# A decode layer in one kernel: the third value product moved ahead of the gate's sum, and the last three rows of w_out in four quarters

## The chip, the cores and the metric

The kernel runs on one core of a Trainium2 chip. The metric is the device time of one execution in microseconds (us), and the figure compared is the median of several runs. A profile is taken of one further execution. Its span, from the first to the last instruction, is shorter than that execution's time, because the time also holds what lies around the program.

## What is computed

One token goes through two branches in parallel, and both results are added to the input. Branch A is attention over the last 4096 positions of a cache with 32 query heads and 16 key and value heads. Branch B is a gated MLP whose gate is normalised over its 2304 values.

```python
xn = _layernorm(x, axis=-1)                       # x: 1 x 1 x 576, bfloat16
return x + _A_ref(xn, k_cache, v_cache, wq, wo) + _B_ref(xn, w_in, w_sp, b_sp, w_out)

# A: W = 4096, 16 heads of 128, each shared by two query heads
q = (xn @ wq).reshape(1, 1, 32, 128)
p = softmax(q . k[last W] * 128 ** -0.5)
A = (p . v[last W]).reshape(1, 1, 4096) @ wo      # wo: 4096 x 576

# B: F/2 = 2304
z = gelu(xn @ w_in)                               # w_in: 576 x 4608
g = w_sp * layernorm(z[..., 2304:]) + b_sp
B = (z[..., :2304] * g) @ w_out                   # w_out: 2304 x 576
```

## The kernel before, in words

All weights and the used part of both caches, 51 MB, are read once. SyncE's queue (SP) issues these loads in a fixed order: wq, k0, k1, v0, k2, v1, k3, win, v2, v3, wo (two parts: rows 0 to 19 and 20 to 31), wout (four parts: rows 0 to 8, 9 to 14, 15 and 16, 17). They share two pools of two buffers each: the small one holds k0, k1, k2, k3, v2 and wout in turn, the large one wq, v0, v1, win, v3 and wo. A load is issued when its buffer is free: wo (L92) when the product with win has been made, wout when k3 has been transposed.

The order of work on each engine is the order in which the program text lists it; no scheduler moves anything. The heads are worked on in four groups of four (b = 0 to 3):

- `turn(b)` (L209): VectorE transposes the group's keys.
- `scores(b)`: TensorE multiplies them with the query (L254), VectorE adds a mask and takes the maximum (L257 to L270), ScalarE takes the exponential (L274), VectorE transposes the probabilities (L276), TensorE sums them (L278, L280).
- `values(b)`: TensorE multiplies the probabilities with the values, 32 matmuls in four column groups into one PSUM tile `pv` (L288). ScalarE copies it to `pvs` (L293). Eight matmuls add up the parts (`op`, L296) and VectorE scales the result into `o_t` (L299).

Then comes branch B. `z_all` multiplies with win in four column groups (L311), and VectorE copies and transposes the result (L315, L317). `gate` is a chain of some fifteen short VectorE and ScalarE operations (L325 to L348), with one matmul in its middle that sums two columns over the partitions (`sz_ps`, L341). Its result `hv` holds 18 columns, one for each row of w_out. The lines around the change are these:

```python
    scores(3)
    gate(z_all())
    values(2)
    values(3)
```

So on TensorE the gate's sum L341 stands ahead of the third values' products, and behind it come the third and the fourth values.

At the end o_t is transposed and reordered into `o_p` (L366 to L370), and all products that make the output are accumulated in PSUM: `row_of` (L376) multiplies one column with one row of weights of 576 values, as two matmuls of 288 columns, the first half into `fin[0]` (partition 0), the second into `fin[1]` (partition 32). It is called once for the input x, 32 times for wo and 18 times for wout, where each part of wout is waited for by the first row that needs it (rows 0, 9, 15 and 17). VectorE casts the one half to bfloat16 (L388), ScalarE the other (L389), and each is written out by a transfer of its own: SP's queue (L390) and ScalarE's queue (L391).

A row (PE) of the profile that says 128*1 is a matmul with 128 partitions and one active column; PEld is the load of that column ahead of it.

Of the kernel before, what the change touches and what calls it, by code (L numbers as in the profile page):

```python
# [8 lines left out]
FP32 = mybir.dt.float32  # L9
BF16 = mybir.dt.bfloat16  # L10
ALU = mybir.AluOpType
# [3 lines left out]
P = 128  # L15
D = 576
# [16 lines left out]
FR = FH // P  # L33
WR = HQ * DH // P
HW = D // 2
ZPAD = 24
ZW = P + ZPAD
SMALL = NU * DH
# [4 lines left out]
def kernel(  # L43
# [14 lines left out]
    nc = tc.nc  # L58
    ctx.enter_context(tc.manual_schedule())

    const = ctx.enter_context(tc.tile_pool(name="const", bufs=1))
    work = ctx.enter_context(tc.tile_pool(name="work", bufs=2))
    one = ctx.enter_context(tc.tile_pool(name="one", bufs=1))
# [7 lines left out]
    ps_a = ctx.enter_context(tc.tile_pool(name="ps_a", bufs=2, space=PS))  # L71
# [11 lines left out]
    def unit(name, width):  # L83
        pool = small if width == SMALL else large
        return pool.tile([P, width], BF16, name=name, tag="u")
# [32 lines left out]
    wout_t = unit("wout", SMALL)  # L118
# [52 lines left out]
    def rstd_of(stats_ps, n, name):  # L171
        mv = const.tile([P, 4], FP32, name=name)
        nc.vector.tensor_scalar_mul(mv[:, 0:2], stats_ps, 1.0 / n)
        nc.vector.tensor_mul(mv[:, 2:3], mv[:, 0:1], mv[:, 0:1])
        nc.vector.tensor_sub(mv[:, 2:3], mv[:, 1:2], mv[:, 2:3])
        nc.scalar.activation(mv[:, 2:3], mv[:, 2:3], ACT.Ln, bias=eps_t[:, 0:1])
        nc.scalar.activation(mv[:, 3:4], mv[:, 2:3], ACT.Exp, scale=-0.5)
        return mv
# [37 lines left out]
    for r in range(NR):  # L216
        for g in range(4):
            nc.tensor.matmul(q_ps[32 * g:32 * g + 32, :], lhsT=xw[:, r, :],  # L218
                             rhs=wq_t[:, 2048 * r + 512 * g:2048 * r + 512 * (g + 1)],
                             start=r == 0, stop=r == NR - 1, tile_position=(0, 32 * g))  # L220
# [5 lines left out]
    for g in range(4):  # L226
        nc.tensor.matmul(qr[:, :, g, :], lhsT=rep4[:, g, :, :].rearrange("p n q -> p (n q)"),
                         rhs=qT[:, :, 0:2, :].rearrange("p a h e -> p h a e"), start=True, stop=True)
    for b in range(NB):
        half, y = divmod(b, 2)  # L230
        nc.vector.tensor_tensor(
            out=zq[:, b, :, ZPAD:].rearrange("p c (n x) -> p c n x", n=4)[:, :, :, 0:8],
            in0=qr[:, half, 2 * y:2 * y + 2, :].rearrange("p g (x c) -> p c (g x)", c=4).unsqueeze(2)
            .to_broadcast([P, 4, 4, 8]),
            in1=qm[:].unsqueeze(1).unsqueeze(3).to_broadcast([P, 4, 4, 8]), op=ALU.mult)
# [10 lines left out]
    def scores(b):  # L246
        sm = one.tile([P, 2, 512], FP32, name=f"sm{b}", tag="sm")
        mx = work.tile([P, 2], FP32, name=f"mx{b}", tag="mx")
        for kk in range(2):
            s_ps = ps_s.tile([P, 512], FP32, name=f"s{b}_{kk}", tag="s")  # L250
            for k4 in range(4):
                for ce in range(4):
                    c, e = divmod(ce, 2)
                    nc.tensor.matmul(s_ps[:], lhsT=zq[:, b, ce, ZPAD - 8 * k4:ZPAD - 8 * k4 + P],  # L254
                                     rhs=kt[b, 4 * kk + k4][:, c, :, e],
# [23 lines left out]
        rms[b] = work.tile([P, 8], FP32, name=f"rm{b}", tag="rm")  # L279
        nc.vector.reciprocal(rms[b][:], su[:])  # L280

    def values(b):
        pv = ps_v.tile([P, 512], FP32, name=f"pv{b}", tag="pv")
        v4 = vn[b][:, 0:NU * DH].rearrange("p (k n u d) -> p k u n d", k=2, n=4, d=DH)
        for kk in range(2):
            for u in range(UK):
                g = u % 4
                nc.tensor.matmul(  # L288
                    pv[32 * g:32 * g + 32, :].rearrange("p (n d) -> p n d", n=4), lhsT=p_t[b][:, kk, u, :],
                    rhs=v4[:, kk, u, :, :], start=kk == 0 and u < 4, stop=kk == 1 and u >= UK - 4,  # L290
                    tile_position=(0, 32 * g))
        pvs = one.tile([P, 512], FP32, name=f"pvs{b}", tag="pvs")
        nc.scalar.copy(pvs[:], pv[:])  # L293
        op = ps_m.tile([P, 8], FP32, name=f"op{b}", tag="m")
        for u in range(4):
            nc.tensor.matmul(op[:], lhsT=pvs[:, DH * u:DH * (u + 1)], rhs=selu[:, 8 * u:8 * u + 8],  # L296
                             start=u == 0, stop=u == 3)
        with nc.allow_low_precision(reason="the attention's output is bfloat16 in the reference"):
            nc.vector.tensor_tensor(out=o_t[:, 8 * b:8 * b + 8], in0=op[:], in1=rms[b][:], op=ALU.mult)  # L299


    hv = const.tile([P, FR], BF16, name="hv")

    def z_all():
        zs = one.tile([P, D], FP32, name="zs", tag="sm")
        zp = [ps_a.tile([P, HW], FP32, name=f"z{i}", tag="a") for i in range(2)]
        for r in range(NR):
            for g in range(4):
                for i in range(2):
                    a = D * g + HW * i  # L310
                    nc.tensor.matmul(zp[i][32 * g:32 * g + 32, :], lhsT=xw[:, r, :],  # L311
                                     rhs=win_t[:, FH * r + a:FH * r + a + HW],
                                     start=r == 0, stop=r == NR - 1, tile_position=(0, 32 * g))
        for i in range(2):
            nc.vector.tensor_copy(zs[:, HW * i:HW * (i + 1)], zp[i][:])  # L315
        zt = one.tile([P, FR, 32], FP32, name="zt", tag="zt")
        nc.vector.transpose(zt[:], zs[:].rearrange("p (i r) -> p r i", r=FR))  # L317
        return zt[:, :, 0:2]

    def gate(z):  # L320
        def t3(name):
            return const.tile([P, FR, 2], FP32, name=name)

        u = t3("u")
        nc.vector.tensor_mul(u[:], z, z)  # L325
        nc.vector.tensor_scalar(out=u[:], in0=u[:], scalar1=0.044715, scalar2=1.0, op0=ALU.mult, op1=ALU.add)
        nc.vector.tensor_mul(u[:], u[:], z)
        nc.vector.tensor_scalar_max(u[:], u[:], -50.0)
        e = t3("e")
        nc.scalar.activation(e[:], u[:], ACT.Exp, scale=-2.0 * GELU_C)  # L330
        nc.vector.tensor_scalar_add(e[:], e[:], 1.0)
        nc.vector.reciprocal(e[:], e[:])
        G = const.tile([P, 2, FR], FP32, name="G")
        nc.vector.tensor_mul(G[:].rearrange("p h c -> p c h"), e[:], z)
        sz = const.tile([P, 2], FP32, name="sz")
        nc.vector.tensor_reduce(out=sz[:, 0:1], in_=G[:, 1, :], axis=AXX, op=ALU.add)
        jz = const.tile([P, FR], FP32, name="jz")
        nc.vector.tensor_tensor_reduce(out=jz[:], in0=G[:, 1, :], in1=G[:, 1, :], scale=1.0, scalar=0.0,
                                       op0=ALU.mult, op1=ALU.add, accum_out=sz[:, 1:2])
        sp = ps_m.tile([P, 2], FP32, name="sz_ps", tag="m")  # L340
        nc.tensor.matmul(sp[:], lhsT=ones_f[:], rhs=sz[:], start=True, stop=True)  # L341
        mz = rstd_of(sp[:], FH, "mz")
        gz = const.tile([P, FR], FP32, name="gz")
        nc.vector.tensor_scalar(out=gz[:], in0=G[:, 1, :], scalar1=mz[:, 0:1], scalar2=mz[:, 3:4],
                                op0=ALU.subtract, op1=ALU.mult)
        nc.vector.tensor_scalar(out=gz[:], in0=gz[:], scalar1=wb[:, 0:1], scalar2=wb[:, 1:2],
                                op0=ALU.mult, op1=ALU.add)
        nc.vector.tensor_mul(hv[:], G[:, 0, :], gz[:])  # L348
# [3 lines left out]
    turn(1)  # L352
    scores(1)
    values(0)
    turn(2)
    scores(2)
    values(1)
    turn(3)
    scores(3)
    gate(z_all())  # L360
    values(2)
    values(3)


# [4 lines left out]
    o_p = const.tile([P, WR], BF16, name="o_p")  # L369
    nc.vector.tensor_copy(o_p[:], op_ps[:])  # L370

    fin = [ps_s.tile([P, HW], FP32, name=f"fin{g}", tag="s") for g in range(2)]

    def row_of(col, w, start=False, stop=False):
        for g in range(2):
            nc.tensor.matmul(fin[g][32 * g:32 * g + 1, :], lhsT=col, rhs=w[:, HW * g:HW * (g + 1)],  # L376
                             start=start, stop=stop, tile_position=(0, 32 * g))

    row_of(one_bf[:, 0:1], x_row, start=True)
    for r in range(WR):  # L380
        row_of(o_p[:, r:r + 1], wo_t[:, D * r:D * (r + 1)])
    for r in range(FR):
        row_of(hv[:, r:r + 1], wout_t[:, D * r:D * (r + 1)], stop=r == FR - 1)


    y = out.flatten_outer_dims()
    res = [const.tile([P, HW], BF16, name=f"res{g}") for g in range(2)]
    nc.vector.tensor_copy(res[0][0:1, :], fin[0][0:1, :])  # L388
    nc.scalar.copy(res[1][32:33, :], fin[1][32:33, :])  # L389
    nc.sync.dma_start(y[:, 0:HW], res[0][0:1, :])  # L390
    nc.scalar.dma_start(y[:, HW:D], res[1][32:33, :])  # L391

# [1 line left out]
_INS = ['A_x', 'A_k_cache', 'A_v_cache', 'A_wq', 'A_wo', 'B_x', 'B_w_in', 'B_w_sp', 'B_b_sp', 'B_w_out']  # L394
# [26 lines left out]
```

## Time and profile before

| what | value |
|---|---|
| time, median of 3 runs | 127.47 us (127.39 to 127.73) |
| time of the profiled execution | 127.53 us |
| span of the profiled execution | 125.7 us |
| mean granted TensorE clock | 0.81 |
| busy: PE, PEld, VectorE (DVE), ScalarE (ACT) | 78.6, 37.6, 64.3, 10.2 us |
| HBM read over the span | 50.96 MB, 405 GB/s |

An engine's busy time is summed over its instructions. The clock is the share of full speed that the throttle granted TensorE. In the timeline, the first column is the start of a group of instructions in us from the span's start, the second how long it lasted; brackets hold the idle time of the engine before it and what ended that. In the chain of waits, each piece of time is given to what the end of the program waited for. In a table of stretches, each engine's busy time comes with the number of its instructions, then the granted clock, the share of the 16 DMA engines and the GB/s.

These lines are from the timeline around the work that the first edit moves:

```profile
92.25 3.82 PE L311 MATMUL z<-win,xw 128*32 128x288 bf16 x72
...
100.63 0.59 PE L341 MATMUL sz_ps<-sz,ones_f 128*128 128x2 f32 x2 [4.55 <-DVE sz L338]
...
101.15 3.60 PE L288 MATMUL pv<-v,pt 128*32 128x512 bf16 x32
...
104.80 0.58 ACT L293 COPY pvs<-pv 128x512 f32<-128x512 f32 x1 [2.44 <-PE pv L288]
...
105.44 1.88 PE L296 MATMUL op<-selu,pvs 128*128 128x8 f32 x8 [0.69 <-ACT pvs L293]
...
107.25 3.30 PE L288 MATMUL pv<-v,pt 128*32 128x512 bf16 x32
```

TensorE ends z at about 96.1 us, idles 4.55 us until the gate's sum, and then does the third and the fourth values, one behind the other.

### The profile page before, as it was taken

Reading aid. Unit: us, or ns where it says so; the run is one execution under the profiler, and the core shown is the slowest. Engines: PE = TensorE matmul, PEld = TensorE weight load, DVE = VectorE, ACT = ScalarE, POOL = GpSimd, SP = SyncE. Lnnn points to the kernel's source line nnn. Section 1 sums busy time; section 2 is a strip of 40 time slices with the busy share of each in tenths; the row PEclk is TensorE's granted clock in tenths of the full one; section 3 lists DMA queues with packets and bytes.
Section 4 is the critical chain, followed back from the end, with each engine's and each line's share of the span. In section 5 each row is a group of like instructions: output and inputs, shape, how many; then the busy total and the mean of one; then the engine's idle time right before and its main releaser. Section 6 shows DMA issues by size and latency. Waiting matters only on the chain.

```text
span 125.7 us, 1318 instructions
## 1 busy us (share of the span) xinstructions
PE 78.6 (62%) x534; PEld 37.6 (30%) x534; DVE 64.3 (51%) x129; ACT 10.2 (8%) x19; POOL 3.9 (3%) x10
## 2 busy tenths in 40 slices
PE   0042750099823998297599646699375097969861
PEld 0032220034211333145234223234063044435540
DVE  6315233499839995330999451999444830010001
ACT  2101000000030000301000031000120011010001
POOL 8400000000000000000000000000000000000000
PEclk9999998559996589755559999689976855595899
DMA  4999899998999989899898999999899999999950
GB/s 102 515 420 438 382 480 438 396 490 365 480 427 394 480 365 490 386 448 469 375 480 386 497 422 422 414 397 480 386 459 443 386 432 442 393 430 411 411 207 0
DMA packets 2467, 51.03 MB, mean 406 GB/s; under 512 B 284, under 2 KB 414, under 8 KB 670
## 3 DMA queue, kind: packets, MB, share of 16 engines
q1 hardware_dynamic: 2450, 50.96, 95.0%
q8 instruction: 4, 0.07, 0.2%
q14 instruction: 1, 0.01, 0.0%
q10 hardware_dynamic: 12, 0.00, 0.0%
HBM read 50.96 MB, written 0.00 MB: 405 GB/s over the span
## 4 chain that ended last, share of the span: by engine, by line
PE 43%; DMA 37%; DVE 10%; ACT 5%; SPq 2%; issue 1%; ACTq 0%
PE s L254 30%; DMA wout<-in_B_w_out_dram 19%; DMA k<-in_A_k_cache_dram 18%; PE pv L288 4%; ACT p L274 4%; DVE kt L209 4%; PE z L311 3%; PE op L296 2%; DVE sm L257 2%; PE tr L265 2%; SPq L92 2%; PE fin L376 1%; PE su L278 1%; DVE pt L276 1%; DVE m L267 1%
## 5 line engine op out<-in xcount | busy, mean ns | idle before, releaser
L254 PE MATMUL s<-kt,zq 128*128 128x512 bf16 x128 | 37.2, 456 | 11.1 <-DVE kt L209 11.1
L209 DVE STREAM_TRANSPOSE kt<-k 128x1024 f32<-128x1024 f32 x32 | 36.4, 1205 | 3.9 <-DMA k<-in_A_k_cache_dram 3.9
L254 PEld LDWEIGHTS <-zq 128*128 128x128 bf16 x128 | 14.4, 112 | 32.8 <-issue 22.1
L288 PE MATMUL pv<-v,pt 128*32 128x512 bf16 x128 | 12.4, 557 | 0.0
L274 ACT ACTIVATE p<-sm,nm 128x1024 bf16<-128x1024 f32 x4 | 4.6, 1147 | 67.9 <-DVE nm L270 67.9
L299 DVE TENSOR_TENSOR o_t<-op,rm 128x8 bf16<-128x8 f32 x4 | 0.7, 166 | 17.2 <-PE op L296 17.2
L276 DVE STREAM_TRANSPOSE pt<-p 128x1024 bf16<-128x1024 bf16 x4 | 5.0, 1245 | 5.4 <-ACT p L274 5.4
L296 PE MATMUL op<-selu,pvs 128*128 128x8 f32 x32 | 5.9, 311 | 2.9 <-ACT pvs L293 2.9
L257 DVE CUSTOM_DVE_ANT_1 sm<-s,cm 128x512 f32<-128x512 f32 x8 | 5.4, 671 | 3.7 <-PE s L254 3.7
L296 PEld LDWEIGHTS op<-selu,pvs 128*128 128x128 f32 x32 | 5.5, 259 | 5.8 <-ACT pvs L293 5.8
L278 PE MATMUL su<-sel,l 128*128 128x8 f32 x8 | 1.8, 293 | 7.6 <-ACT p L274 7.6
L218 PE MATMUL q_ps<-wq,xw 128*32 128x512 bf16 x36 | 4.2, 626 | 3.0 <-DVE xw L187 2.4
L376 PE MATMUL fin<-wo,o_p 128*1 128x288 bf16 x64 | 5.8, 357 | 0.1
L156 PE MATMUL x_ps<-one_bf,x_row 1*64 1x1 bf16 x9 | 1.2, 248 | 7.4 <-DMA x_row<-in_A_x_dram 7.4
L288 PEld LDWEIGHTS <-pt 128*32 128x32 bf16 x128 | 4.0, 128 | 5.6 <-issue 4.8
L388 DVE CAST res<-fin 1x288 bf16<-1x288 f32 x1 | 0.4, 446 | 9.9 <-PE fin L376 9.9
L265 PE MATMUL tr<-ident_f,m 128*128 128x128 f32 x8 | 1.9, 326 | 3.9 <-DVE m L263 3.9
L376 PEld LDWEIGHTS <-o_p 128*1 128x1 bf16 x64 | 3.4, 103 | 2.3 <-DVE o_p L370 0.3
L278 PEld LDWEIGHTS su<-sel,l 128*128 128x128 f32 x8 | 1.4, 218 | 8.4 <-ACT p L274 8.4
L311 PE MATMUL z<-win,xw 128*32 128x288 bf16 x72 | 3.8, 392 | 0.0
L376 PE MATMUL fin<-wout,hv 128*1 128x288 bf16 x36 | 2.6, 285 | 1.5 <-DMA wout<-in_B_w_out_dram 1.5
L293 ACT COPY pvs<-pv 128x512 f32<-128x512 f32 x4 | 2.3, 585 | 14.3 <-PE pv L288 14.3
(88 smaller groups left out, 39.0 us busy)
## 6 DMA issues: line engine op xcount, KB each, us to landing
k<-in_A_k_cache_dram SPq DMA_DIRECT2D x4, 4096.0 KB
v<-in_A_v_cache_dram SPq DMA_DIRECT2D x4, 4096.0 KB, 39.0
win<-in_B_w_in_dram SPq DMA_DIRECT2D x1, 5184.0 KB
wq<-in_A_wq_dram SPq DMA_DIRECT2D x1, 3584.0 KB
wo<-in_A_wo_dram SPq DMA_DIRECT2D x1, 2880.0 KB
wo<-in_A_wo_dram SPq DMA_DIRECT2D x1, 1728.0 KB, 20.0
wout<-in_B_w_out_dram SPq DMA_DIRECT2D x1, 1296.0 KB
wq<-in_A_wq_dram SPq DMA_DIRECT2D x1, 1024.0 KB, 4.9
```

Source lines behind the costliest of these rows:

```text
L209: nc.vector.transpose(t[:].rearrange("p c n e -> p (c n e)").bitcast(FP32), kn[b][:, UK * DH * k:UK * DH * (k + 1)].bitcast(FP32).rearrang ...
L218: nc.tensor.matmul(q_ps[32 * g:32 * g + 32, :], lhsT=xw[:, r, :], rhs=wq_t[:, 2048 * r + 512 * g:2048 * r + 512 * (g + 1)], start=r == 0, ...
L254: nc.tensor.matmul(s_ps[:], lhsT=zq[:, b, ce, ZPAD - 8 * k4:ZPAD - 8 * k4 + P], rhs=kt[b, 4 * kk + k4][:, c, :, e], start=k4 == 0 and ce = ...
L257: nc.vector.tensor_tensor_reduce(out=sm[:, kk, :].rearrange("p (n s) -> p n s", s=HB), in0=s_ps[:].rearrange("p (n s) -> p n s", s=HB), in ...
L265: nc.tensor.matmul(tr[:], lhsT=m1[:].to_broadcast([P, P]), rhs=ident_f[:], start=True, stop=True)
L274: nc.scalar.activation(p[:], sm[:].rearrange("p k n -> p (k n)"), ACT.Exp, bias=nm[:], accum_out=l[:])
L276: nc.vector.transpose(p_t[b][:].rearrange("p k u m -> p (k u m)"), p[:])
L278: nc.tensor.matmul(su[:], lhsT=l[:].to_broadcast([P, P]), rhs=sel8[:], start=True, stop=True)
L288: nc.tensor.matmul(pv[32 * g:32 * g + 32, :].rearrange("p (n d) -> p n d", n=4), lhsT=p_t[b][:, kk, u, :], rhs=v4[:, kk, u, :, :], start=k ...
L296: nc.tensor.matmul(op[:], lhsT=pvs[:, DH * u:DH * (u + 1)], rhs=selu[:, 8 * u:8 * u + 8], start=u == 0, stop=u == 3)
L311: nc.tensor.matmul(zp[i][32 * g:32 * g + 32, :], lhsT=xw[:, r, :], rhs=win_t[:, FH * r + a:FH * r + a + HW], start=r == 0, stop=r == NR - ...
L376: nc.tensor.matmul(fin[g][32 * g:32 * g + 1, :], lhsT=col, rhs=w[:, HW * g:HW * (g + 1)], start=start, stop=stop, tile_position=(0, 32 * g))
```

## The change

`values` is split into `weigh` (the products and ScalarE's copy) and `heads` (the eight matmuls and the scaling). For group 2, `weigh` is called between `z_all` and `gate`, and `heads` behind `gate`. Groups 0, 1 and 3 keep both together.

The last three rows of w_out (LATE = 3: rows 15, 16 and 17) no longer accumulate into `fin`. Its accumulation stops at row 14. The four quarters of `fin`, 144 columns each, are copied into a tile `sums` in SBUF, at partitions 0, 32, 64 and 96: two copies on VectorE, two on ScalarE. The three rows are multiplied in four quarters each, twelve matmuls of 144 columns in four column groups, into a tile `last` in PSUM at the same four partitions. One VectorE operation over 128 partitions adds the two tiles and casts to bfloat16; both tiles are filled with zeros before, as only four of their partitions are written. Each of the two output transfers now writes two rows of 144 values (288 bytes), taken from two partitions.

```diff
-    def values(b):
+    def weigh(b):
         pv = ps_v.tile([P, 512], FP32, name=f"pv{b}", tag="pv")
...
         nc.scalar.copy(pvs[:], pv[:])
+        return pvs
+
+    def heads(b, pvs):
         op = ps_m.tile([P, 8], FP32, name=f"op{b}", tag="m")
...
+    def values(b):
+        heads(b, weigh(b))
...
-    gate(z_all())
-    values(2)
+    z = z_all()
+    pvs2 = weigh(2)
+    gate(z)
+    heads(2, pvs2)
     values(3)
...
+    last = ps_a.tile([P, QW], FP32, name="last", tag="a")
+    nc.vector.memset(last[:], 0.0)
+    sums = one.tile([P, QW], FP32, name="sums", tag="pvs")
+    nc.vector.memset(sums[:], 0.0)
...
-    for r in range(FR):
-        row_of(hv[:, r:r + 1], wout_t[:, D * r:D * (r + 1)], stop=r == FR - 1)
...
-    nc.vector.tensor_copy(res[0][0:1, :], fin[0][0:1, :])
-    nc.scalar.copy(res[1][32:33, :], fin[1][32:33, :])
-    nc.sync.dma_start(y[:, 0:HW], res[0][0:1, :])
-    nc.scalar.dma_start(y[:, HW:D], res[1][32:33, :])
+    for r in range(FR - LATE):
+        row_of(hv[:, r:r + 1], wout_t[:, D * r:D * (r + 1)], stop=r == FR - LATE - 1)
+    for c in range(2):
+        nc.vector.tensor_copy(sums[32 * c:32 * c + 1, :], fin[0][0:1, QW * c:QW * (c + 1)])
+        nc.scalar.copy(sums[64 + 32 * c:65 + 32 * c, :], fin[1][32:33, QW * c:QW * (c + 1)])
+    for r in range(FR - LATE, FR):
+        for c in range(4):
+            nc.tensor.matmul(last[32 * c:32 * c + 1, :], lhsT=hv[:, r:r + 1],
+                             rhs=wout_t[:, D * r + QW * c:D * r + QW * (c + 1)],
+                             start=r == FR - LATE, stop=r == FR - 1, tile_position=(0, 32 * c))
+
+    y = out.flatten_outer_dims().rearrange("o (c n) -> (o c) n", c=4)
+    res = const.tile([P, QW], BF16, name="res")
+    nc.vector.tensor_tensor(out=res[:], in0=last[:], in1=sums[:], op=ALU.add)
+    nc.sync.dma_start(y[0:2, :], res[0:64:32, :])
+    nc.scalar.dma_start(y[2:4, :], res[64:128:32, :])
```

More of the change, by code (lines that the diff above doesn't have):

```diff
@@ L35 @@
 HW = D // 2
+QW = D // 4
+LATE = 3
 ZPAD = 24
@@ L381 @@
         row_of(o_p[:, r:r + 1], wo_t[:, D * r:D * (r + 1)])
-    for r in range(FR):
-        row_of(hv[:, r:r + 1], wout_t[:, D * r:D * (r + 1)], stop=r == FR - 1)
[L386 to L390, printed above, removed]
-    nc.scalar.dma_start(y[:, HW:D], res[1][32:33, :])
+    for r in range(FR - LATE):
[13 more added lines that the diff above has]
+    nc.scalar.dma_start(y[2:4, :], res[64:128:32, :])
 _INS = ['A_x', 'A_k_cache', 'A_v_cache', 'A_wq', 'A_wo', 'B_x', 'B_w_in', 'B_w_sp', 'B_b_sp', 'B_w_out']
```

## The prediction

> **What bounds the kernel now.** I read the page's queue table first, then the chain of work that ended last, then the tail of the timeline.
>
> ```profile
> DMA packets 2467, 51.03 MB, mean 406 GB/s; under 512 B 284, under 2 KB 414, under 8 KB 670
> ## 3 DMA queue, kind: packets, MB, share of 16 engines
> q1 hardware_dynamic: 2450, 50.96, 95.0%
> q8 instruction: 4, 0.07, 0.2%
> ```
>
> SP's queue (q1) keeps 16 engines busy for 95% of the span: the kernel is one stream of 51 MB. The chain from 90 us on shows where it ends:
>
> ```profile
> 92.33 3.81 PE z L311 x72
> ...
> 97.48 24.29 DMA wout<-in_B_w_out_dram
> 121.78 0.04 issue
> 121.82 1.39 PE fin L376 x18
> 123.21 0.43 DVE res L388
> ```
>
> Between 97.5 and 121.8 only w_out's transfer stands on the path. What PE, VectorE and ScalarE do there is off it while it is done before the part of w_out that it needs. The tail, from the timeline:
>
> ```profile
> 113.32 5.76 PE L376 MATMUL fin<-wo,o_p 128*1 128x288 bf16 x64
> ...
> 119.71 1.27 PE L376 MATMUL fin<-wout,hv 128*1 128x288 bf16 x18 [0.64 <-DMA wout<-in_B_w_out_dram]
> ...
> 121.82 1.35 PE L376 MATMUL fin<-wout,hv 128*1 128x288 bf16 x18 [0.84 <-DMA wout<-in_B_w_out_dram]
> ...
> 123.20 0.45 DVE L388 CAST res<-fin 1x288 bf16<-1x288 f32 x1 [9.94 <-PE fin L376]
> 123.23 0.39 ACT L389 CAST res<-fin 1x288 bf16<-1x288 f32 x1 [11.99 <-PE fin L376]
> ...
> 123.67 0.31 SPq L390 DMA_DIRECT2D out_dram<-res  x1
> ```
>
> PE waits 0.64 us for rows 0 to 8 and 0.84 us for rows 9 to 17. The second group is 0.08 us longer than the first although it is the same work; the stretches of 0.04 us show why (columns: PE, PEld, DVE, ACT, POOL, clock, DMA):
>
> ```profile
> 122.50:122.54 0.04, 0.04 (x4) 0.01 (x1) 0.00 (x0) 0.00 (x0) 0.00 (x0) 1.00 0.00 0
> 122.54:122.58 0.04, 0.04 (x4) 0.00 (x0) 0.00 (x0) 0.00 (x0) 0.00 (x0) 1.00 0.00 0
> 122.58:122.62 0.04, 0.04 (x6) 0.03 (x3) 0.00 (x0) 0.00 (x0) 0.00 (x0) 1.00 0.00 0
> ```
>
> Weight loads stop and start again at 122.58: row 15 had to wait for w_out's third part. The trace's DMA records have the four parts landing at 119.67, 121.78, 122.54 and 122.84, and PE's records start row 17 at 122.88. So the last rows already run as they land, and the fixed end is 122.84 plus one row, one cast and the output.
>
> **First edit: third values ahead of the gate's sum.** It moves 32 matmuls, 32 weight loads and one ScalarE copy from 101.15 to behind z's last matmul, beside VectorE's gate chain (96.12 to 100.57). v2 lands at 95.80, so they start at 95.84. The clock table says at what speed (PE alone):
>
> ```profile
> 96.46:99.87 3.41, 0.00 (x0) 1.00 0.99 418
> 99.87:103.28 3.41, 2.65 (x26) 0.50 0.92 395
> ...
> 113.52:116.94 3.42, 3.42 (x32) 0.50 1.00 418
> 116.94:120.35 3.41, 2.77 (x46) 1.00 0.97 391
> 120.35:123.76 3.41, 1.98 (x30) 1.00 0.25 95
> ```
>
> The clock changes in steps of 3.41 us and follows the work of the stretch before: after the idle 96.46:99.87 it halves, after the full 113.52:116.94 it doubles. From 96.46 it is full, so the group takes about 2.4 us (1.87 us at full clock and 3.60 us at half clock in the chain's and timeline's pv rows) and ends at 98.2; all at half clock it ends at 99.4. L341's sum needs PE at 100.62: covered either way. Behind the pvs copy on ScalarE is queued the gate's exp (due 99.16); at full clock the copy is done at 98.9, at half clock the exp is 0.9 us late and hv is ready at 104.1 instead of 103.2, needed at 119.7. No DMA is moved: wo's issue waits for z's last matmul, w_out's for the last k.
>
> What comes earlier: the fourth values. They need v3, whose landing is SP's idle end at 105.5 (123.6 minus the 18.1 us that SP then waits for res), so they start at 105.5, not 107.25. The wo rows start when o_p is there or wo's first part (landing 112.36): 112.4 to 112.7, not 113.32. wo's second part lands at 116.52, so the rows end between 118.2 and 118.9, not 119.08. Then PE waits for w_out at 119.67 as before, 0.8 to 1.5 us instead of 0.64. Worth nothing on the path. If that cover were gone (w_out landing over 0.64 us sooner), the edit would be worth the rest, up to 0.9 us.
>
> **Second edit: the tail.** Rows 9 to 14 run as now: last pair starts at 122.43, ends 0.285 later, 122.72. Then four steps.
>
> Copies. VectorE starts 0.03 behind PE (123.17 to 123.20), at 122.75. A 1x144 copy lies between L370's 128x32 (0.192) and L388's 1x288 (0.446): 0.30 in between. L315's pair takes 0.82 at 0.452 each, so the second overlaps by 0.08 and ends at 122.75 + 0.22 + 0.30 = 123.27. ScalarE starts 0.06 behind PE, at 122.78; between 128x36 (0.233) and 1x288 (0.389), 0.26 to 0.30 each: 123.32.
>
> Quarter matmuls. L311's z has the same four column groups: four start within some 0.03 us, the next four 0.21 to 0.24 later, at half clock and 288 columns. A quarter of that is 0.06 for a row of four at 144 columns. Rows 15 and 16 run from 122.58 to 122.70, row 17 starts at 122.88 as before and ends after 0.22 (between 0.176 for 32 columns, L368, and 0.285): 123.10. If instead each costs z's mean pace (3.82/72 = 0.053), twelve from 122.58 end at 123.39. I take 123.10, as the records show four starting together.
> The Trainium skill, "TensorE: Matmul & The Clock Gate", section "Wait — 56ns, not 53.3ns?", gives small matmuls a floor of about 62 ns each where the sequencer decodes them in microcode. By it the twelfth would start at 123.26, SP issue at 123.86 and the kernel lose 0.16 us more; by z's four starts in 0.03 us the floor does not bind here.
>
> Add. It waits for all three: 123.32, plus 0.05. L231's 128x128 with a operand in PSUM takes 0.282, so 0.30: ends 123.67 (at the 1x288 cast's 0.446, 123.82). SP issues 0.03 later: 123.70, against 123.67. So the shorter last operation (0.15) and matmul (0.06) are spent on the copies, which stand bare for 0.2 us behind PE.
>
> The two memsets (a 128x128 one takes 0.165, L131) lie where VectorE idles 9.94 us.
>
> Output. Two transfers as before, each of two pieces of 288 B in place of one of 576 B. No row has such a write. Lower bound 0: pieces run on two engines beside each other. Upper bound 0.43: SP's piece starts at 124.47 and lands at 124.90 in the trace's records, and a piece that cost that stretch twice would land so much later. I take 0, as x_row's 384 B pieces take 20 to 22 ns of an engine, the 576 B pieces 27.
>
> Sum: 127.53 for the profiled execution (125.7 span plus 1.8 around it) + 0.03 = 127.56; it stood 0.06 above the median, so **127.5**. Ends: copies at their lower rows (VectorE 123.13, ScalarE 123.25), add at 0.28: SP at 123.61, minus 0.06. Copies at 0.446 without overlap: 123.64, add 0.446: SP at 124.17, plus 0.50.
>
> **Rivals.**
>
> A, slower: the small output pieces. Place: behind the add, nothing covers it, SP ends the program only when both have landed. Price up to 0.43: 127.53 + 0.03 + 0.43 = 128.0. It decides from 0.35 us on. For it: 284 packets on the page are under 512 B, and none is an output of 288 B, so nothing shows it free. Against: the engines' times per small piece above.
> The Trainium skill, "DMA: Bandwidth & Descriptors", Specifications, states 512 B as the smallest transfer at line rate, with a read-modify-write below it. No run here shows a write below it; by that rule this rival holds.
>
> B, slower: bare copies. All at the 1x288 price, one behind the other, as worked out: 128.0. It decides when copies and add take over 1.27 us from 122.75 (I have 0.92). Against: L315's pair overlaps.
>
> C, slower: the clock. A matmul of 288 columns starts every 0.06 us in the rows at full clock, every 0.12 at half (28 starts in 113.52:116.94). Should the stretch before 121.8 be too idle, twelve matmuls take 0.72 more: 127.56 + 0.72 = 128.3. PE waits longer before w_out now. Against: that stretch still holds some 1.7 us of wo rows and 0.6 us of w_out's, and 1.98 busy of 3.41 us left the clock full.
>
> D, faster: executions whose clock steps lie elsewhere. Where before ran all 64 wo rows at half clock (64 x 0.12 = 7.7 us, to 121.0), w_out's first 18 matmuls would end at 122.1 and the end slip by some 0.5 us; the first edit removes that: 127.56 - 0.5 = 127.1 against the same execution of before. Against: three times within 0.34 us show no such one.
>
> E, slower: one more instruction fetch. Each of the page's four q8 packets holds one engine for about 1.0 us (4.9% of 16 engines over 118.2 to 119.5), and w_out's last parts wait for such engines. A fifth on one already late: 128.6. Against: 990 PE records precede the last, some 90 follow, now 102, and they were 215 or more apart.
>
> **How the numbers follow.** Forecast, no change: 0.56, time 127.5, own range 127.3 to 127.85. A 0.11, B 0.10, C 0.04, E 0.03: slower 0.28. D 0.16: faster. Bound: 0.3% of 127.47 is 0.38 us, about what can be told from no change. Range: 127.1 reaches D, 128.1 the ends of A and B; under 2 in 10 is left out.
>
> **What would show it.** Right: pv of the third values near 95.9, x18 fin rows at 119.7, x12 at 121.8, twelve quarter matmuls ending near 123.1, two copies each on VectorE and ScalarE to about 123.3, SP's issue at 123.6 to 123.8. Wrong: copies that end after 123.6, a landing of out over 1.4 us after SP's issue, a half clock after 120, or w_out's last part off 122.84 by over 0.3 us.

## The result, and the profile after

The changed kernel takes 128.69 us in the median of 5 runs (128.15 to 128.95), against 127.47 us (127.39 to 127.73, now 5 runs). The ratio, estimated from the single executions, is 1.0078 with a 95% interval of 1.0052 to 1.0104 (the two medians alone would give 1.0096): slower by just under 1%. The profiled execution took 128.28 us with a span of 126.5 us, so 0.75 us more than the profiled execution before in both. Three of the five executions lie between 128.69 and 128.95 us, longer than any that was profiled, so the profiles account for 0.75 of the 1.22 us between the two medians; when the kernel was measured again (`after_again` below), its median lay 0.69 us above the kernel before.

The tail of the timeline, changed kernel (PE, VectorE, ScalarE and the two queues, start and length in us):

```profile
121.80 0.90 PE L391 MATMUL fin<-wout,hv 128*1 128x288 bf16 x12 [0.75 <-DMA wout<-in_B_w_out_dram]
...
122.56 0.58 PE L404 MATMUL last<-wout,hv 128*1 128x144 bf16 x12
122.73 0.61 DVE L400 COPY sums<-fin 1x144 f32<-1x144 f32 x2 [10.68 <-PE fin L391]
122.77 0.55 ACT L401 COPY sums<-fin 1x144 f32<-1x144 f32 x2 [13.13 <-PE fin L391]
...
123.47 0.31 DVE L410 TENSOR_TENSOR res<-last,sums 128x144 bf16<-128x144 f32 x1
123.81 0.63 SPq L411 DMA_DIRECT2D out_dram<-res  x1
123.81 0.57 ACTq L412 DMA_DIRECT2D out_dram<-res  x1
```

Up to SP's issue little is lost: 123.81 against 123.67. But the issue itself now lasts 0.63 us on SP and 0.57 on ScalarE's queue, where it lasted 0.31 and 0.22. What follows takes longer still, as SP's wait at the end shows (engine and line, what it waited for, us in total, times, longest). Changed kernel:

```profile
SPq L437 <- DMA out_dram<-res: 1.0, 2, 0.7
```

and the kernel before:

```profile
SPq L416 <- DMA out_dram<-res: 0.5, 1, 0.5
```

The trace's records of the transfers give the rest; a piece is one run of bytes that a transfer moves in one packet. SP's output landed 1.23 us after the start of its issue (123.67 to 124.90); now it lands 1.84 us after it (123.81 to 125.65). So of the 0.75 us, 0.14 lie ahead of the issue and 0.61 behind its start: 0.32 in the issue, 0.37 more from its end to the first piece (124.44 to 125.30; before 123.98 to 124.47), and 0.08 less from that piece to the landing (125.30 to 125.65; before 124.47 to 124.90).

The first edit did its part, and it reached nothing. TensorE's rows around it:

```profile
95.84 1.91 PE L290 MATMUL pv<-v,pt 128*32 128x512 bf16 x32 [0.27 <-DMA v<-in_A_v_cache_dram]
...
105.56 3.44 PE L290 MATMUL pv<-v,pt 128*32 128x512 bf16 x32 [3.66 <-DMA v<-in_A_v_cache_dram]
...
112.41 5.77 PE L391 MATMUL fin<-wo,o_p 128*1 128x288 bf16 x64 [0.77 <-DMA wo<-in_A_wo_dram]
119.79 1.27 PE L391 MATMUL fin<-wout,hv 128*1 128x288 bf16 x18 [1.61 <-DMA wout<-in_B_w_out_dram]
```

The third values start at 95.84 and the fourth at 105.56, when v3 is there. The wo rows start 0.9 us sooner than before, and all of it turns into waiting for w_out: 1.61 us instead of 0.64.

### The profile page after: what moved, and what is told of

The parts are those of the page before. It is cut to its first block, busy times and chain, and to the rows that moved or that the text cites. A ratio compares the mean times of both kernels' runs of the same rounds, so it can differ in the third digit from the quotient of the medians.

```text
span 126.5 us, 1334 instructions
## 1 busy us (share of the span) xinstructions
PE 74.5 (59%) x536; PEld 36.4 (29%) x540; DVE 65.0 (51%) x133; ACT 10.3 (8%) x20; POOL 3.9 (3%) x10
## 4 chain that ended last, share of the span: by engine, by line
PE 42%; DMA 37%; DVE 10%; ACT 5%; issue 2%; SPq 2%; ACTq 0%; DVEq 0%
PE s L256 29%; DMA wout<-in_B_w_out_dram 20%; DMA k<-in_A_k_cache_dram 18%; PE pv L290 4%; ACT p L276 4%; DVE kt L211 4%; PE op L301 3%; DVE sm L259 2%; PE z L319 2%; PE tr L267 2%; SPq L94 2%; DVE pt L278 1%; DVE m L269 1%; ACT pvs L295 1%; PE su L280 1%
## 5 line engine op out<-in xcount | busy, mean ns | idle before, releaser
L290 PE MATMUL pv<-v,pt 128*32 128x512 bf16 x128 | 10.7, 493 | 3.9 <-DMA v<-in_A_v_cache_dram 3.9
L400 DVE COPY sums<-fin 1x144 f32<-1x144 f32 x2 | 0.6, 296 | 10.7 <-PE fin L391 10.7
L158 PEld LDWEIGHTS <-x_row 1*64 1x64 bf16 x9 | 1.1, 204 | 7.3 <-issue 7.3
```

Of the source, the lines that this page charges most:

```text
L290: nc.tensor.matmul(pv[32 * g:32 * g + 32, :].rearrange("p (n d) -> p n d", n=4), lhsT=p_t[b][:, kk, u, :], rhs=v4[:, kk, u, :, :], start=k ...
```

## The experiments

Two theories were set against each other. Theory O: the output transfers cost the time. Theory S: the moved matmuls disturb the stream (instruction fetches, clock), so that w_out lands later. Every ratio below is to the kernel before, measured beside it on the same chip, where its median was 127.66 to 127.69 us. A diff is against the kernel before, unless the text says that it is against the changed one.

**One edit at a time.** `weigh_only` has the first edit alone, with `values` split as in the change:

```diff
-    gate(z_all())
-    values(2)
+    z = z_all()
+    pvs2 = weigh(2)
+    gate(z)
+    heads(2, pvs2)
```

> The kernel before with the first edit alone (third values ahead of the gate's sum; tail and output as before). Theory O (the output transfers of two pieces each cost the time, first their issue, then their landing): no change, 127.4 to 127.6 us, spread of the times as before (0.35 us). Theory S (the earlier matmuls move TensorE's instruction fetches or clock, and w_out's last part lands later in some executions): 127.9 to 128.3 us in the median and a spread of over 0.6 us.

Measured: 127.65 us in 11 runs, ratio 0.9998 (0.9989 to 1.0006). That is 0.05 us above Theory O's range, as the kernel before itself, at 127.66, was on this chip. The first edit is worth nothing, and Theory S falls for it.

`tail_only` has the second edit alone (diff against the changed kernel):

```diff
-    z = z_all()
-    pvs2 = weigh(2)
-    gate(z)
-    heads(2, pvs2)
+    gate(z_all())
+    values(2)
```

> The kernel before with the second edit alone (last three rows in quarters, add, output in pieces of 288 B; third values where they were). Theory O: 128.2 to 128.9 us, as the whole change, with SP's issue of out at 0.6 us instead of 0.3 and landing over 1.7 us after its start. Theory S: 127.5 to 127.8 us.

Measured: 128.40 us, ratio 1.0062 (1.0046 to 1.0078); issue 0.63 us, landing 1.86 us after its start. The loss is in the tail, as Theory O has it; which part of the tail, the next two runs ask.

**The output alone.** `out_quarters` keeps all 18 rows in two halves and changes what follows them:

```diff
...
-    nc.vector.tensor_copy(res[0][0:1, :], fin[0][0:1, :])
-    nc.scalar.copy(res[1][32:33, :], fin[1][32:33, :])
-    nc.sync.dma_start(y[:, 0:HW], res[0][0:1, :])
-    nc.scalar.dma_start(y[:, HW:D], res[1][32:33, :])
...
+    for c in range(2):
+        nc.vector.tensor_copy(res[32 * c:32 * c + 1, :], fin[0][0:1, QW * c:QW * (c + 1)])
+        nc.scalar.copy(res[64 + 32 * c:65 + 32 * c, :], fin[1][32:33, QW * c:QW * (c + 1)])
+    nc.sync.dma_start(y[0:2, :], res[0:64:32, :])
+    nc.scalar.dma_start(y[2:4, :], res[64:128:32, :])
```

> The kernel before, all rows in two halves as there; only the output changes: two casts of 144 values on VectorE and two on ScalarE into four partitions, and each queue writes two pieces of 288 B. Theory O: 0.17 us for the second casts (two of 0.30 one behind the other for one of 0.446) and 0.6 us for the transfers, so 128.2 to 128.9 us; SP's issue lasts 0.6 us. If the add and the copies of the change cost more than the output: 127.6 to 127.9 us.

```profile
123.81 0.64 SPq L392 DMA_DIRECT2D out_dram<-res  x1
```

Measured: 128.48 us, ratio 1.0063 (1.0051 to 1.0075). Without quarter matmuls and without an add, a loss as large is there. Of it, 0.13 us lie ahead of SP's issue (123.81 against 123.67, the second casts), the rest behind.

**The add without the pieces.** `halves_add` is the other side: the last rows, copies and add stay, but in two halves, so that each transfer is one piece of 576 B (against the changed kernel).

```diff
-    last = ps_a.tile([P, QW], FP32, name="last", tag="a")
+    last = ps_a.tile([P, HW], FP32, name="last", tag="a")
...
-        for c in range(4):
+        for c in range(2):
...
-    nc.sync.dma_start(y[0:2, :], res[0:64:32, :])
-    nc.scalar.dma_start(y[2:4, :], res[64:128:32, :])
+    nc.sync.dma_start(y[:, 0:HW], res[0:1, :])
+    nc.scalar.dma_start(y[:, HW:D], res[32:33, :])
```

> The changed kernel with the last three rows, the copies and the add in two halves of 288 columns in place of four quarters, so that each output transfer is one piece of 576 B as before; first edit kept. Theory O-count (a second piece in a transfer costs, the add does not): copies end at 123.20, the add (some 0.45 us) at 123.75, SP's issue lasts 0.31 us and lands 1.23 us after its start: 127.7 to 127.8 us where before has 127.66, a ratio of 1.000 to 1.001. If the copies and the add are the larger part of the loss: 1.004 or more.

Its timeline's end:

```profile
122.54 0.60 PE L403 MATMUL last<-wout,hv 128*1 128x288 bf16 x6
122.75 0.45 DVE L399 COPY sums<-fin 1x288 f32<-1x288 f32 x1 [10.09 <-PE fin L391]
...
123.32 0.45 DVE L409 TENSOR_TENSOR res<-last,sums 33x288 bf16<-33x288 f32 x1
123.80 0.32 SPq L410 DMA_DIRECT2D out_dram<-res  x1
123.81 0.23 ACTq L411 DMA_DIRECT2D out_dram<-res  x1
```

Measured: 127.62 us in 11 runs, ratio 0.9994 (0.9984 to 1.0003). That is a little under the 127.7 us expected. SP's issue starts as late as in the changed kernel (123.80), but lasts 0.32 us, and the loss is gone. In this profile the output still lands 0.16 us later than in that of the kernel before (125.06 against 124.90); the medians show no such loss. So copying and adding is neutral within what the runs can tell, and with `out_quarters` the loss is pinned on transfers of several pieces.

**Size, count or partitions?** Three kernels ask which property of the pieces it is. `pieces_576` is the kernel before with its two halves as two pieces of one transfer:

```diff
-    y = out.flatten_outer_dims()
...
-    nc.sync.dma_start(y[:, 0:HW], res[0][0:1, :])
-    nc.scalar.dma_start(y[:, HW:D], res[1][32:33, :])
+    y = out.flatten_outer_dims().rearrange("o (c n) -> (o c) n", c=2)
+    res = const.tile([P, HW], BF16, name="res")
+    nc.vector.tensor_copy(res[0:1, :], fin[0][0:1, :])
+    nc.scalar.copy(res[32:33, :], fin[1][32:33, :])
+    nc.sync.dma_start(y[:, :], res[0:64:32, :])
```

> The kernel before, with its two halves of 576 B as two pieces of one transfer from SP (two partitions of one tile). If a piece under 512 B is what costs (Theory O-size): SP's issue 0.31 us, 127.5 to 127.8 us. If more than one piece in a transfer is what costs, whatever its size (Theory O-count): SP's issue 0.6 us, landing 1.6 us after its start, 127.9 to 128.2 us.

```profile
123.19 0.45 DVE L388 CAST res<-fin 1x288 bf16<-1x288 f32 x1 [10.35 <-PE fin L376]
123.22 0.39 ACT L389 CAST res<-fin 1x288 bf16<-1x288 f32 x1 [13.23 <-PE fin L376]
123.70 0.63 SPq L390 DMA_DIRECT2D out_dram<-res  x1
```

Measured: 127.96 us, ratio 1.0016 (1.0004 to 1.0028). The casts are those of before, the pieces have their old size, and the issue takes 0.63 us. So the long issue does not come from the size. The loss of 0.28 us is under half of the changed kernel's: this kernel issues one transfer from one queue, and the table below shows what a second queue adds.

`pieces_one_partition` leaves the two transfers of before, each in two pieces of 288 B out of one partition:

```diff
...
-    nc.sync.dma_start(y[:, 0:HW], res[0][0:1, :])
-    nc.scalar.dma_start(y[:, HW:D], res[1][32:33, :])
...
+    res = [const.tile([P, 2, QW + 16], BF16, name=f"res{g}") for g in range(2)]
...
+    nc.sync.dma_start(y[:, 0:2, :], res[0][0:1, :, 0:QW])
+    nc.scalar.dma_start(y[:, 2:4, :], res[1][32:33, :, 0:QW])
```

> The kernel before, with each of its two transfers in two pieces of 288 B that lie in one partition (a gap of 32 B between them); casts as before but for the gap. Theory O-count: issues of 0.6 us and 128.2 to 128.6 us, as the second edit alone. If it is the two partitions that cost (Theory O-partition): issues of 0.31 and 0.22 us and 127.5 to 127.8 us.

```profile
123.73 0.68 ACTq L392 DMA_DIRECT2D out_dram<-res  x1
123.75 0.74 SPq L391 DMA_DIRECT2D out_dram<-res  x1
```

Measured: 128.38 us, ratio 1.0056 (1.0043 to 1.0069). It is not the two partitions either: with both pieces in one partition the issues are no shorter, 0.74 and 0.68 us.

`one_queue` is the changed kernel with its four pieces in one transfer from SP (against the changed kernel):

```diff
-    nc.sync.dma_start(y[0:2, :], res[0:64:32, :])
-    nc.scalar.dma_start(y[2:4, :], res[64:128:32, :])
+    nc.sync.dma_start(y[:, :], res[0:128:32, :])
```

> The changed kernel with one output transfer of four pieces from SP in place of two transfers of two pieces from two queues. If the two queues' issues hold each other up (Theory O1): the issue is no longer than 0.6 us, landing under 1.6 us after its start, 127.9 to 128.3 us. If each piece costs its own 0.3 us (Theory O2): an issue of 1.2 us, landing 2.4 us after its start, 128.9 to 129.5 us. Theory S: as the changed kernel, 128.7 us, with the same spread.

```profile
123.89 0.65 SPq L411 DMA_DIRECT2D out_dram<-res  x1
```

Measured: 128.25 us, ratio 1.0046 (1.0033 to 1.0059). Four pieces are issued in 0.65 us, two in 0.63: the step is from one piece to several, not per piece. O1's time came; its two bounds, 0.6 us for the issue and 1.6 for the landing, were both passed by some 0.05 us. The landing, 1.66 us after the start of the issue, comes 0.19 sooner than with two queues.

`four_transfers` issues the four pieces of the changed kernel one by one (against it):

```diff
-    nc.sync.dma_start(y[0:2, :], res[0:64:32, :])
-    nc.scalar.dma_start(y[2:4, :], res[64:128:32, :])
+    for c in range(2):
+        nc.sync.dma_start(y[c:c + 1, :], res[32 * c:32 * c + 1, :])
+        nc.scalar.dma_start(y[2 + c:3 + c, :], res[64 + 32 * c:65 + 32 * c, :])
```

> The changed kernel with its four pieces of 288 B as four transfers of one piece each, two on each queue. Theory O-count (a transfer of several pieces is issued on a slower way, a transfer of one piece is not): two issues of 0.31 us one behind the other on SP and two of 0.22 on ScalarE's queue, the last landing 0.3 + 1.2 us after the first issue starts: 127.95 to 128.15 us, 0.2 to 0.4 us faster than the change. If the cost comes with the number of pieces, however they are issued: 128.3 to 128.5 us, as the change.

Measured: 128.17 us, ratio 1.0041 (1.0025 to 1.0057), just above the range expected. SP's two issues last 0.32 and 0.27 us, and the second lands 1.22 us after its own start, where a piece of 576 B took 1.23. A lone piece of 288 B costs nothing extra; the second transfer pays for standing 0.37 us behind the first.

**One piece.** `one_piece` goes the other way: both casts into one partition, one transfer of 1152 B from ScalarE's queue.

```diff
-    res = [const.tile([P, HW], BF16, name=f"res{g}") for g in range(2)]
-    nc.vector.tensor_copy(res[0][0:1, :], fin[0][0:1, :])
-    nc.scalar.copy(res[1][32:33, :], fin[1][32:33, :])
-    nc.sync.dma_start(y[:, 0:HW], res[0][0:1, :])
-    nc.scalar.dma_start(y[:, HW:D], res[1][32:33, :])
+    res = const.tile([P, D], BF16, name="res")
+    nc.vector.tensor_copy(res[0:1, 0:HW], fin[0][0:1, :])
+    nc.scalar.copy(res[0:1, HW:D], fin[1][32:33, :])
+    nc.scalar.dma_start(y[:, :], res[0:1, :])
```

> The kernel before, with both casts into one partition and one transfer of one piece of 1152 B from ScalarE's queue. By before's rows ScalarE's issue takes 0.22 us and lands 1.07 us after its start, SP's 1.23: the end comes up to 0.15 us earlier, 127.45 to 127.65 us where before has 127.66. If the two issues at once do not hold each other up: no change.

Measured: 127.63 us in 12 runs, ratio 1.0001 (0.9993 to 1.0009). It lands 1.10 us after the start of its issue, about as expected, but the issue starts 0.08 us after VectorE's cast ends (123.69 to 123.77), and no gain can be told. From the end of its issue to its first packet pass 0.49 us, as on each of the two queues before: two transfers of one piece do not hold each other up. No version here beats the kernel before by more than its measurement can tell.

**The changed kernel again.** `after_again` is the changed kernel, unaltered, and so are `spread_1` and `spread_2`, one profiled execution each.

> The changed kernel once more, beside the others on one chip. The first edit alone gave 0.9998 and the second alone 1.0062 of before. If that is all (Theory O): 1.005 to 1.009 of before, a spread of up to 0.8 us, and in every profile SP's issue at about 0.6 us and a landing over 1.7 us after its start. If the two edits together have a cost of their own (Theory S): over 1.009, with w_out's last part landing after 123.3 us.

Measured: 128.37 us in 6 runs (128.25 to 129.03), ratio 1.0064 (1.0046 to 1.0082). SP's issue lasts 0.63 us, out lands 1.85 us after its start, w_out's last part at 122.95. The two edits together cost what the second costs alone.

> The changed kernel, one profile, to catch one of its slower executions (128.7 to 129.0 us instead of 128.2 to 128.5). In a slower one Theory O has SP's issue start at 123.7 to 123.9 us as in the others and the landing of out over 2.2 us later. Theory S has w_out's last part landing at over 123.3 us instead of 122.9, from two instruction fetches on one engine.

> The same once more: Theory O, in a slower execution, out lands over 2.2 us after the start of SP's issue; Theory S, w_out's last part lands at over 123.3 us.

They took 128.32 and 128.39 us, so neither caught a longer one; both have the issue at 0.63 us, the landing 1.85 us after its start, w_out's last part at 122.93 and 122.97. What makes some executions longer, `after_again`'s 129.03 us and `tail_only`'s 128.87 among them, stays open: no profile shows such a one. The kernel before has one too, 128.45 us among the 23 beside `after_again`.

All outputs side by side, from the traces' records (one profile each; us):

| kernel | transfers x pieces | issue on SP, ScalarE's queue | from the start of the first issue to the last landing |
|---|---|---|---|
| before | 2 x 1 of 576 B | 0.31, 0.22 | 1.25 |
| halves_add | 2 x 1 of 576 B | 0.32, 0.23 | 1.26 |
| one_piece | 1 x 1 of 1152 B | -, 0.23 | 1.10 |
| four_transfers | 4 x 1 of 288 B | 0.32 and 0.27, 0.23 and 0.26 | 1.60 |
| pieces_576 | 1 x 2 of 576 B | 0.63, - | 1.61 |
| one_queue | 1 x 4 of 288 B | 0.65, - | 1.66 |
| changed kernel | 2 x 2 of 288 B | 0.63, 0.57 | 1.84 |
| out_quarters | 2 x 2 of 288 B | 0.64, 0.56 | 1.92 |
| pieces_one_partition | 2 x 2 of 288 B | 0.74, 0.68 | 2.05 |

On one queue two pieces of 576 B and four of 288 B differ by 0.05 us; with two queues it is 0.19 us and more on top.

## Why the prediction was wrong

The forecast was no change, 127.5 us, and it failed in one step: **the output**. I took 0 for it and 0.43 us as its upper bound. It measured 0.61 in the profile, and the sign that the prediction itself named for being wrong, a landing over 1.4 us after SP's issue, came with 1.84. Both numbers came from what the pieces do on the DMA engines: their packets (20 to 27 ns) and the way from packet to landing. That part was right, and even fell (0.43 to 0.35 us). What I left out is the issue. An issue had been on the page all along as a row of 0.31 us, I carried it over unchanged though its transfer had changed shape, and so the bound from above held only the part behind the packet. The doubled issue (0.32 more) and the longer way to the first packet (0.37 more) have no place in my sum. The further 0.4 us or so in the first median are not explained by any profile; the forecast would have failed without them too, as no execution took under 128.15 us.

**Rival A** had the right place and the right sign, and a chance of 0.11; its price, 128.0 us, was under even the fastest run of 128.15. Its mechanism, the small size, is refuted: pieces of 576 B in one transfer cost the same issue, and a lone piece of 288 B lands as fast as one of 576 B. The Trainium skill's rule that I put beside it ("DMA: Bandwidth & Descriptors", Specifications: a read-modify-write below 512 B) shows no cost here: the way from packet to landing became shorter, 0.35 us instead of 0.43.

**First edit.** Right in the starts that carry it: third values from 95.84, fourth from 105.56, wo rows from 112.41 (112.4 to 112.7 forecast), w_out's first rows at 119.79, nothing gained. Two sizes were off without consequence: the third values took 1.91 us, all at full clock, where I had 2.4 from a mixture of both clocks, and TensorE waited 1.61 us for w_out, where I had 0.8 to 1.5.

**Copies.** VectorE's end came at 123.34 and ScalarE's at 123.31; I had 123.27 and 123.32. The term that was off is the overlap. I took 0.08 us from L315's pair, but the second copy starts 0.31 us after the first, which lasts 0.30: no overlap in any of these kernels.

**Quarter matmuls.** Four start together, the next four 0.06 us later, each lasts 0.22 us, and the last ends at 123.14; I had 123.10. The floor of about 62 ns that the Trainium skill gives for matmuls decoded in microcode ("TensorE: Matmul & The Clock Gate", "Wait — 56ns, not 53.3ns?") is not seen: the twelve starts take 0.35 us, 0.27 of it the wait for row 17.

**Add.** 0.31 us where I had 0.30. From the last copy's end to its start pass 0.13 us (123.34 to 123.47), where I had 0.05. SP's issue starts at 123.81; I had 123.70, so +0.14 instead of +0.03. B, the bare copies at 0.446 each, did not come.

**C, D and E.** These are the clock's table for the changed kernel, from 112.10 on (PE, granted clock, DMA share, GB/s):

```profile
112.10:115.52 3.42, 3.11 (x28) 0.50 0.97 413
115.52:118.93 3.41, 2.64 (x40) 1.00 1.00 415
118.93:122.34 3.41, 1.81 (x28) 1.00 0.65 253
```

Its edges lie elsewhere than before (115.52 instead of 116.94), yet the stretch of the tail is at full clock: C did not come. My reason against C was weak all the same. I took it from one stretch with 1.98 us busy, but in the kernel before the stretch 110.11:113.52, with 2.08 us busy, was followed by half clock, so TensorE's busy time alone does not tell. D, a gain in executions with other edges, was not paid either: `weigh_only` and the kernel before have medians of 127.65 and 127.66 us over 11 and 17 runs, whose mean clocks run from 0.78 to 0.85. E did not come: the page still counts four instruction fetches.

```profile
q8 instruction: 4, 0.07, 0.2%
```

and w_out's last part lands at 122.86, against 122.84, in the profiled execution.

The range ended at 128.1 because its upper end was built from bounds of the terms I had listed. An operation that was not listed had no bound.

## What to carry to other kernels

When a change alters the shape of a transfer, cost the whole instruction again: its issue, the way from the issue to the first packet, and the landing. At the end of a kernel, where nothing covers the output, one piece for each transfer was worth 0.3 to 0.7 us here over the same bytes in two pieces (`pieces_576`, `pieces_one_partition`); splitting the last work over four partitions brought SP's issue no sooner (123.81 against 123.67) and left the pieces behind. And a stage that ends with a load stream gained nothing here from an earlier start of the work in front of it: look at what the wait in front of the last load grows by.

## What was unexpected in the hardware

An output transfer of several pieces was issued in 0.63 to 0.65 us on SP whether it had two pieces or four, each from a partition of its own (0.74 us for two from one partition), and in 0.31 or 0.32 us if it had one. The number of pieces does not set this by itself. The loads of w_out, each into 128 partitions, are issued on the same queue in about 0.4 us, all but one (shortest, median and longest in ns):

```profile
L92 SPq DMA_DIRECT2D wout<-in_B_w_out_dram x4: 382/430/1229, 97.1 to 99.2; - x4
```

Why two pieces of an output take longer to issue than a load into 128 partitions was not tried, and is open.

With two queues issuing transfers of two pieces at once, SP's first piece moved 0.86 us after the end of its issue (124.44 to 125.30), 0.27 us behind those of ScalarE's queue. With SP alone it moved after 0.60 us, both for four pieces of 288 B (124.54 to 125.14) and for two of 576 B (124.33 to 124.93), so neither the size nor the number makes the difference. That the two queues hold each other up is read from these times and from 0.19 us between the landings of the changed kernel and `one_queue`; two against one queue with the same transfer was not tried by itself.

The four engines that end the stream late were not tried either. In the kernel before, eleven of sixteen engines finish w_out's last part by 121.5 us, one at 122.1 and four between 122.7 and 122.84. Four packets of 16 KB of instructions held an engine for about 1.0 us each in the same span. Whether the one makes the other is open.
